# Memory attention and a feed-forward layer on one core: the order of all steps written anew

## The chip, the cores and the metric

One core of a Trainium2 chip runs the whole program. The metric is the device time of one execution in microseconds (us); the number given for a kernel is the median of its runs.

## The reference, cut to what matters

```python
def attention(q, k, v, phi):                 # 8 batches, 8 heads, 576 rows, 64 wide, 32 memories
    a = softmax(phi, axis=2)                 # over the 576 rows
    k_m = einsum('bhsm,bhsd->bhmd', a, k)
    v_m = einsum('bhsm,bhsd->bhmd', a, v)
    attn = softmax((q @ k_m.T) / 8, axis=-1) # over the 32 memories
    return attn @ v_m

def ffn(x, w_in, w_out):                     # x: 4608 x 512, w_in: 512 x 2048, w_out: 2048 x 512
    h = x @ w_in
    return maximum(0.01 * h, h) @ w_out

out = ffn(heads side by side of attention(q, k, v, phi), w_in, w_out)
```

q, k, v and phi are float32. w_in and w_out arrive as 64-bit floating-point numbers.

## The kernel before

**Folding.** The kernel never forms the attention's output. v_m of a batch is multiplied into w_in first (`fold_products`, L896), so that a batch's feed-forward layer takes its 256 attention weights per row straight to the 2048 hidden columns. Operands of most products are split into two float16 parts, and three of the four partial products are kept.

**Named steps.** Every piece of work is a function in the dictionary `steps`, under a short name. Two strings, OPENING (L39) and LATER (L68), list all names once; `run` calls them in that order. No scheduler changes it: each engine (PE, DVE, ACT, POOL, and SP, which issues the transfers) executes its own instructions in the order in which the strings bring them, and waits only for data or for a buffer. Of two steps on different engines, the order in the string means nothing unless one needs the other's result or its buffer.

**The names.** `a0.` to `a7.` are the attention steps of a batch. `phi`, `k`, `v`, `kv0` to `kv3`, `q0`, `q1` load (SP, L535, L546, L566). `A1` (DVE maximum over phi, L575), `A2` (PE transpose, L589), `A3`, `B0`, `B10` (subtract), `B20` (ACT exponential, L620), `B3` (sum), `C10` and `C11` (PE, k_m and v_m, L654), `C2` (PE), `C30` (DVE, L677 to L682), `C3k` (ACT, x_k, L689), `C31` (DVE, x_v, L700), `C4` (DVE, a diagonal of maxima, mdiag, L341), `D10` and `D11` (PE transposes, L719 and L727), `D3` (ACT copy kT, L736), `D2` (PE spread of mdiag, L346), `D4`, `D5`, `D6` (v's scale and its two parts), `Q0`, `Q1` (DVE transposes of q, L772), `E10` and `E1` (PE scores, L793), `E20` to `E22` (DVE transposes out of PSUM, L807), and `S01` to `S18` (softmax over the memories, the chunks 0 and 1).

`i0.` to `i3.` and `o0.` to `o3.` are the quarters of w_in and w_out, each in three pieces of 768, 768 and 512 columns: `ld` (load, L374), `y` and `h` (the high and the low word of the 64-bit number, on ACT, L395 and L384, some `h` on DVE, as OPENING_ACT says), `t` (DVE joins them to float32, L404), `b` (squares for a bound, ACT, L409). Later `k`, `l`, `s`, `m`, `n` split these and their sums into float16.

`f00.` to `f03.` (L909, copied by ACT at L1244) fold the first batch's v_m into a quarter of w_in. `u0.` to `u7.` are eight units of the first group of rows: `P` (PE, L993), `V` (leaky step on ACT, L1000), `O` (PE, L1061). `ci.` and `co.` work out scales of w_in and w_out. `P8` to `P23`, with `V`, `C`, `L`, `O`, are the next two groups; `Wbj` are folded weights (L909, L932, L938). `p0` to `p55` are the units of the remaining fourteen groups: `p` (PE, L1104), `v` (ACT, L1120), `s` (DVE, L1141), `c` (ACT, L1145), `l` (DVE, L1149), and, one or two units later, `d` (PE, L1172). `x` and `z` combine and store.

**Idle products.** `z.4`, `z.1`, `z.3` of the opening (`idle_products`, L1257) are that many 128 by 512 float32 products of ones, whose result nobody reads.

**What limits the order.** PSUM gives the attention steps three banks (`ps_a`), the products `P` and `p` two and the products `O` and `d` three. `ld_slot` (L304) hands out eight buffers in turn, so a load waits until the load eight before it has been worked off. Eight semaphores tell of landings: SP waits with a ninth transfer until the first has landed.

```python
IDLE = (1, 3, 4)

def load(i):                       # one piece of a quarter of w_in or w_out
    c0, n = PIECES[i]
    st = ld_slot().bitcast(I64)
    x = c0
    while x < c0 + n:
        m = min(FQ - x % FQ, c0 + n - x)
        nc.sync.dma_start(st[:, x - c0:x - c0 + m], src[:, x // FQ, x % FQ:x % FQ + m])
        x += m

def squares():
    nc.scalar.activation(junk, dst, AF.Square, scale=SQ_SCALE, accum_out=sq[:, col])
```

Of the kernel before, what the change touches and what calls it, by code (L numbers as in the profile page):

```python
# [45 lines left out]
o1.y0 u1.P1 a0.S16 i2.ld0 o0.t2 a0.S17 u1.V0 u0.O0 a0.S18 i2.ld1 u1.V1 i1.y0 i1.h0 o1.y1 i1.t0  # L46
o1.h0 u1.O0 i1.h1 i1.y1 o1.t0 i1.y2 i1.t1 i2.ld2 i1.h2 u0.O1 o1.h1 i1.t2 i2.h0 i2.y0 o1.t1
o1.y2 i2.t0 o2.ld0 o1.h2 f01.1 i2.y1 i2.h1 u1.O1 o1.t2 f01.2 i2.t1 o2.ld1 o2.ld2 a1.phi i2.y2
i2.h2 o2.y0 u2.P0 i2.t2 a1.kv0 o2.h0 f02.1 u2.V0 o2.t0 o2.y1 a1.kv1 u2.P1 f02.2 u3.P0 a1.kv2
u2.V1 o2.h1 u3.P1 u3.V0 o2.t1 a1.kv3 o2.y2 u2.O0 a1.A1 u3.V1 o2.h2 i1.b a1.q0 o2.t2 a1.A2 u4.P0  # L50
a1.A3 i2.b a1.q1 a1.B0 u4.P1 a1.B10 u4.V0 o0.b u3.O0 i3.ld0 a1.B20 u5.P0 u4.V1 a1.B3 o1.b
a1.C10 u5.V0 o2.b u5.P1 i3.ld1 i3.ld2 o3.ld0 a1.Q0 a1.C2 u2.O1 a1.Q1 u5.V1 i3.y0 a1.C30 i3.h0
a1.C3k u3.O1 a1.C31 i3.y1 i3.h1 a1.C4 i3.y2 i3.h2 i3.t0 a1.D10 a1.D11 i3.t1 a1.D3 a1.D2 u4.O0
a1.D5 a1.D4 o3.y0 i3.t2 o3.h0 i3.b o3.t0 a1.E1 u5.O0 o3.ld1 o3.ld2 a1.E20 a1.E21 a1.S01 a1.E22
a1.S02 a1.S11 ci.1 a1.S03 f03.1 ci.2 a1.S04 a1.S12 o3.y1 ci.3 u4.O1 f03.2 ci.4 e. a1.S05 a1.S13
w0.2 o3.h1 u6.P0 o3.y2 o3.h2 a1.S06 u6.P1 a1.S14 u6.V0 a1.S07 u7.P0 u6.V1 a1.S08 o3.t1 u7.P1
u7.V0 o3.t2 a1.S15 w1.1 o3.b u6.O0 w1.2 u7.V1 a1.S16 co.1 u7.O0 co.2 a1.S17 a1.S18 co.3 u5.O1
# [16 lines left out]
o1.m0 W03.l1 W03.l0 O10.0 V12.0 L11 o0.n3 P12.1 o1.n0 o1.s1 O10.1 V12.1 a2.A3 o1.m1 o1.s2 o1.n1
W13.p o1.m2 C12 a2.B0 o1.s3 W13.h1 P13.0 W13.h0 W13.l1 P13.1 W13.l0 V13.0 o2.k1 L12 P14.0 V13.1
o1.n2 O11.0 o2.k0 o2.l1 V14.0 o2.l0 o2.k2 P14.1 o1.m3 o2.l2 C13 O11.1 V14.1 o1.n3 L13 P15.0
o2.s0 C14 o2.m0 O12.0 o2.s1 V15.0 o2.n0 o2.m1 L14 P15.1 o2.n1 O12.1 o2.s2 V15.1 a2.B10 o2.m2
P16.0 o2.s3 a2.B20 C15 O13.0 o2.n2 V16.0 o3.k0 L15 o3.k1 o3.s0 a2.C10 o3.l0 o3.k2 o2.m3 o3.l1
P16.1 o3.l2 a2.q1 a2.q0 o3.s1 O13.1 V16.1 a2.B3 P17.0 C16 a3.phi a2.C2 o3.s2 V17.0 O14.0 L16
o3.m2 o3.m3 a2.C30 o3.m1 P17.1 o3.n2 a2.C3k o3.n1 O14.1 o3.m0 o3.n3 V17.1 a2.Q0 a2.D10 P18.0  # L80
C17 a2.D3 a2.Q1 O15.0 V18.0 L17 P18.1 a2.C31 i0.l2 a2.E1 V18.1 a2.C4 C18 i0.l1 O15.1 a3.kv3
a3.kv2 a3.kv0 a3.kv1 L18 a2.E20 P19.0 Z1.0 a2.E22 a2.E21 Z1.1 a2.D2 i0.l0 a2.D11 Z1.2 V19.0
a2.S01 O16.0 i1.k0 i1.k1 a2.D4 P19.1 i1.k2 a2.S02 a2.D5 O16.1 V19.1 a2.D6 a2.S03 i1.l2 C19
W20.p i1.l1 P20.0 L19 W20.h0 W20.h1 O17.0 a2.S04 V20.0 P20.1 W20.l0 a2.S05 O17.1 V20.1 C20
a2.S06 P21.0 L20 O18.0 a2.S07 W20.l1 i1.l0 V21.0 a2.S08 P21.1 o2.n3 i2.k0 W21.p V21.1 O18.1
# [6 lines left out]
p2.0 v1.3 Z2.0 os3 p2.1 s1 Z2.2 d0.0 v2.0 d0.1 c1.0 d0.2 v2.1 l1.0 c1.1 p2.2 d0.3 v2.2 l1.1
a3.D5 d0.4 p2.3 a3.D6 a4.A1 a3.E1 v2.3 c2.0 l2.0 d0.5 a4.kv2 a4.kv0 a4.kv3 a4.kv1 d0.6 s2 p3.0
p3.1 v3.0 a3.E20 d1.0 a3.E22 v3.1 c2.1 d1.1 a3.E21 d1.2 l2.1 W30.p p3.2 a3.S01 W30.h0 d1.3 v3.2
W30.h1 d1.4 W30.l0 a3.S02 p3.3 W31.p v3.3 W30.l1 c3.0 d1.5 d1.6 a3.S03 l3.0 p4.0 s3 p4.1 v4.0
d2.0 v4.1 d2.1 a3.S04 c3.1 d2.2 W31.h1 p4.2 d2.3 l3.1 v4.2 W31.h0 d2.4 a3.S05 p4.3 d2.5 v4.3
W31.l0 d2.6 c4.0 W31.l1 p5.0 l4.0 p5.1 v5.0 s4 d3.0 v5.1 d3.1 x3.p a4.A2 a3.S06 d3.2 c4.1 p5.2
l4.1 d3.3 v5.2 a3.S07 d3.4 x3.0 p5.3 x3.1 d3.5 a3.S08 v5.3 x3.2 d3.6 c5.0 a4.A3 p6.0 x3.3 a4.B0
v6.0 l5.0 p6.1 z3.0 d4.0 v6.1 z3.1 d4.1 s5 d4.2 p6.2 a4.B10 c5.1 d4.3 d4.4 v6.2 l5.1 a4.B20
p6.3 d4.5 v6.3 a4.B3 a4.C10 c6.0 l6.0 d4.6 a4.q0 a4.q1 a5.phi s6 a4.C2 p7.0 p7.1 v7.0 a4.C30  # L100
d5.0 v7.1 c6.1 d5.1 a4.C31 d5.2 a4.C3k l6.1 p7.2 a4.D10 v7.2 a4.C4 d5.3 a4.D3 a4.Q0 d5.4 p7.3
a5.A1 d5.5 v7.3 d5.6 c7.0 p8.0 p8.1 l7.0 v8.0 d6.0 s7 v8.1 d6.1 d6.2 a4.Q1 c7.1 p8.2 d6.3 v8.2
a4.D2 l7.1 d6.4 p8.3 a4.D4 a4.D11 v8.3 d6.5 os4 c8.0 W32.p a4.D5 l8.0 d6.6 W32.h1 p9.0 W32.h0
a4.D6 W32.l1 p9.1 v9.0 W32.l0 d7.0 v9.1 s8 a4.E1 x4.p c8.1 d7.1 a5.kv0 a5.kv2 a5.kv1 a5.kv3
l8.1 d7.2 p9.2 x4.0 d7.3 v9.2 a4.E21 d7.4 x4.1 p9.3 x4.2 d7.5 a4.E22 v9.3 d7.6 c9.0 a4.E20
p10.0 x4.3 W33.p l9.0 v10.0 p10.1 s9 W33.h0 d8.0 v10.1 W33.h1 d8.1 W33.l0 c9.1 d8.2 W33.l1
p10.2 l9.1 d8.3 v10.2 z4.1 d8.4 a4.S01 z4.0 p10.3 d8.5 v10.3 W40.p c10.0 d8.6 W40.h1 l10.0
p11.0 W40.h0 s10 p11.1 v11.0 d9.0 v11.1 d9.1 a4.S02 c10.1 d9.2 p11.2 l10.1 d9.3 v11.2 W40.l1
a4.S03 d9.4 W40.l0 p11.3 a4.S04 d9.5 v11.3 W41.p c11.0 d9.6 W41.h1 l11.0 p12.0 W41.h0 s11 p12.1
v12.0 d10.0 v12.1 d10.1 a4.S05 c11.1 d10.2 p12.2 l11.1 d10.3 v12.2 a4.S06 d10.4 p12.3 W41.l0  # L110
d10.5 v12.3 W41.l1 d10.6 c12.0 p13.0 l12.0 a5.A2 v13.0 p13.1 s12 d11.0 v13.1 d11.1 x5.p a5.A3
d11.2 c12.1 p13.2 l12.1 a5.B0 v13.2 d11.3 a4.S07 x5.0 d11.4 p13.3 x5.1 a4.S08 x5.2 d11.5 v13.3
d11.6 c13.0 p14.0 x5.3 p14.1 l13.0 v14.0 d12.0 v14.1 z5.0 d12.1 s13 z5.1 d12.2 p14.2 a5.B10
c13.1 d12.3 d12.4 v14.2 l13.1 a5.B20 p14.3 d12.5 v14.3 a5.B3 a5.C10 c14.0 l14.0 d12.6 a6.phi
a5.q0 a5.q1 s14 a5.C2 p15.0 p15.1 v15.0 a5.C30 d13.0 v15.1 c14.1 d13.1 a5.C31 d13.2 a5.C3k
l14.1 p15.2 a5.D10 v15.2 a5.C4 d13.3 a5.D3 a5.Q0 d13.4 p15.3 a6.A1 d13.5 v15.3 d13.6 c15.0
p16.0 p16.1 l15.0 v16.0 d14.0 s15 v16.1 d14.1 d14.2 a5.Q1 c15.1 a5.D2 p16.2 a5.D11 v16.2 d14.3
l15.1 d14.4 a5.D4 p16.3 d14.5 v16.3 W42.p c16.0 os5 d14.6 W42.h0 l16.0 p17.0 W42.h1 W42.l0
p17.1 v17.0 W42.l1 d15.0 v17.1 s16 d15.1 x6.p a5.D5 d15.2 p17.2 c16.1 x6.0 d15.3 a5.D6 v17.2
l16.1 a5.E1 x6.1 d15.4 a6.kv1 a6.kv0 a6.kv2 a6.kv3 a5.E21 p17.3 x6.2 d15.5 a5.E22 v17.3 d15.6  # L120
c17.0 a5.E20 p18.0 x6.3 W43.p l17.0 v18.0 p18.1 s17 W43.h1 d16.0 v18.1 W43.h0 d16.1 W43.l1
# [1236 lines left out]
```

## Time and profile before

| | us |
|---|---|
| median of 3 runs | 666.64 (666.6 to 666.78) |
| the profiled execution's own time | 668.56 |
| its span, first to last instruction | 666.0 |
| PE busy in the span | 644.3 |
| DVE busy | 515.2 |
| ACT busy | 398.6 |

The profiled execution takes 1.92 us longer than the median, 2.56 us of it outside its span. Differences between two kernels are worked out within the span and then laid on the median. PE is busy almost throughout, so the time is read from the few stretches in which PE stands still or runs at its lower clock, and from what ends them.

### The profile page before, as it was taken

Reading aid. Unit: us, or ns where it says so; the run is one execution under the profiler, and the core shown is the slowest. Engines: PE = TensorE matmul, PEld = TensorE weight load, DVE = VectorE, ACT = ScalarE, POOL = GpSimd, SP = SyncE. Lnnn points to the kernel's source line nnn. Section 1 sums busy time; section 2 is a strip of 40 time slices with the busy share of each in tenths; the row PEclk is TensorE's granted clock in tenths of the full one; section 3 lists DMA queues with packets and bytes.
Section 4 is the critical chain, followed back from the end, with each engine's and each line's share of the span. In section 5 each row is a group of like instructions: output and inputs, shape, how many; then the busy total and the mean of one; then the engine's idle time right before and its main releaser. Section 6 shows DMA issues by size and latency. Waiting matters only on the chain.

```text
span 666.0 us, 17554 instructions
## 1 busy us (share of the span) xinstructions
PE 644.3 (97%) x7592; PEld 483.1 (73%) x7592; DVE 515.2 (77%) x857; ACT 398.6 (60%) x677; POOL 29.8 (4%) x43
## 2 busy tenths in 40 slices
...
GB/s 257 400 317 306 239 170 49 1 1 110 188 1 53 103 144 33 109 144 33 10 132 36 142 1 33 5 104 177 33 14 79 15 33 8 27 20 16 33 2 47
DMA packets 32604, 60.37 MB, mean 91 GB/s; under 512 B 4368, under 2 KB 14608, under 8 KB 32528
## 3 DMA queue, kind: packets, MB, share of 16 engines
...
q8 instruction: 59, 0.97, 0.6%
...
## 4 chain that ended last, share of the span: by engine, by line
PE 84%; DMA 8%; DVE 4%; ACT 1%; SPq 1%; issue 1%; DVEq 0%; ACTq 0%
PE po L1172 28%; PE ph L1104 20%; PE po L1061 13%; PE ph L993 8%; PE ph L1172 5%; PE pa L909 4%; DMA arena<-in_q_dram 3%; PE pa L654 2%; PE pa L793 2%; DMA arena<-in_moe_w_in_dram 2%; PE po L1206 1%; DMA wi<-in_v_dram 1%; DMA arena<-in_phi_dram 1%; DMA arena<-in_moe_w_out_dram 1%; DVE arena L772 1%; DVE r1k L575 1%
## 5 line engine op out<-in xcount | busy, mean ns | idle before, releaser
L1172 PEld LDWEIGHTS <-arena 128*128 128x128 f16 x2184 | 209.8, 98 | 32.0 <-issue 9.0
L1120 ACT ACTIVATE wi<-ph,g_sc 128x256 f32<-128x256 f32 (+1 forms) x224 | 99.8, 465 | 167.2 <-PE ph L1104 166.3
L1104 PE MATMUL ph<-a,w_mem 128*128 128x256 f16 (+3 forms) x1440 | 147.1, 247 | 3.3 <-ACT wi L1120 3.1
L1104 PEld LDWEIGHTS <-w_mem 128*128 128x128 f16 x1440 | 115.4, 98 | 18.3 <-issue 6.7
L1172 PE MATMUL po<-wo,arena 128*128 128x256 f16 x936 | 122.5, 273 | 0.0
L1172 PE MATMUL po<-arena 128*128 128x256 f16 x936 | 121.9, 273 | 0.0
L1061 PE MATMUL po<-wo,arena 128*128 128x512 f16 (+1 forms) x384 | 110.7, 434 | 0.0
L1149 DVE TENSOR_TENSOR arena<-arena 128x1024 f16<-128x1024 f32 x52 | 63.2, 1216 | 27.7 <-ACT arena L1145 27.6
L1149 DVE TENSOR_TENSOR arena<-wi,arena 128x768 f16<-128x768 f32 (+1 forms) x60 | 52.9, 882 | 31.5 <-ACT arena L1145 31.3
L1145 ACT CAST arena<-arena 128x1024 f16<-128x1024 f32 x52 | 54.2, 1043 | 10.5 <-DVE arena L1141 10.2
L993 PE MATMUL ph<-a,w_mem 128*128 128x192 f16 (+2 forms) x304 | 53.8, 323 | 1.7 <-DVE a L852 1.7
L1141 DVE TENSOR_TENSOR arena<-wi 128x256 f32<-128x256 f32 x104 | 39.2, 418 | 15.3 <-ACT wi L1120 15.3
L1061 PEld LDWEIGHTS <-arena 128*128 128x128 f16 x288 | 27.8, 98 | 29.3 <-issue 0.9
L1145 ACT CAST arena<-wi 128x768 f16<-128x768 f32 (+1 forms) x60 | 46.5, 775 | 1.8
L1141 DVE TENSOR_TENSOR arena<-wi,arena 128x256 f32<-128x256 f32 x104 | 43.8, 422 | 1.8
L1172 PE MATMUL ph<-wo,arena 128*128 128x256 f16 x312 | 42.6, 273 | 0.0
L876 POOL TENSOR_TENSOR a<-t,a 128x384 f16<-128x384 f32 x22 | 21.4, 997 | 450.9 <-ACT a L871 380.4
L1061 PEld LDWEIGHTS po<-wo,arena 128*128 128x128 f32 x96 | 17.6, 190 | 21.0 <-issue 19.1
L772 DVE STREAM_TRANSPOSE arena<-arena 96x1536 f32<-96x1536 f32 x14 | 24.7, 1766 | 8.0 <-DMA arena<-in_q_dram 3.7
L1000 ACT ACTIVATE arena<-ph,g_sc 128x384 f32<-128x384 f32 x32 | 18.5, 578 | 18.3 <-PE ph L993 17.6
L909 PE MATMUL pa<-wi,vT 64*32 64x512 f16 (+1 forms) x704 | 29.0, 420 | 0.4 <-ACT vT L742 0.4
L993 PEld LDWEIGHTS <-w_mem 128*128 128x128 f16 x240 | 20.8, 98 | 9.3 <-issue 2.7
...
## 6 DMA issues: line engine op xcount, KB each, us to landing
...
```

The costliest lines, as they stand in the source:

```text
L772: nc.vector.transpose(flat, ld["q", g].rearrange("p hh j d -> p (hh j d)"))
L876: nc.gpsimd.tensor_tensor(lo[:, tb], t2[:, tb], hi[:, tb], ALU.subtract)
L909: nc.tensor.matmul(pf[g][cols, :], lhs, rhs, start=(n == 0), stop=(n == len(passes) - 1), tile_position=(g * D, hh * M),)
L993: nc.tensor.matmul(ph[:, t0:t0 + n * SB], lhs, rhs, start=(m == 0), stop=(m == len(seq) - 1))
L1000: nc.scalar.activation(dst, ph, AF.Prelu, scale=sc, alpha=SLOPE)
L1061: nc.tensor.matmul(po, lhs, rhs, start=(f == 0 and m == 0), stop=(f == NQ * NF - 1 and m == len(seq) - 1),)
L1104: nc.tensor.matmul(ph[:, t0:t0 + n], lhs, rhs, start=(m == 0), stop=(m == len(seq) - 1))
L1120: nc.scalar.activation(dst, ph, AF.Prelu, scale=g_sc2[:, j:j + 1], alpha=SLOPE)
L1141: nc.vector.tensor_tensor(gt[:, x], y, z, op)
L1145: nc.scalar.copy(dst[:, 0], src)
L1149: nc.vector.tensor_tensor(dst[:, 1], src, dst[:, 0], ALU.subtract)
L1172: nc.tensor.matmul(acc, g[:, x, s, u], rhs, start=(h == 0 and j == 0 and u == 0 and m == 0), stop=(j == NQ - 1 and u == 1 and m == 2), ski ...
```

## The change

Only the two strings and IDLE change. No step is taken away or altered; the one new step is `z.2`, two idle products behind `f00.1` and ahead of `u0.P0`. The core of the diff:

```diff
 OPENING = """
-z.4 a0.phi0 a0.phi1 a0.k a0.q0 a0.A10 a0.A11 a0.A2 a0.q1 a0.A3 a0.B0 z.1 a0.B10 a0.B11 a0.B20
-i0.ld0 a0.B21 a0.C10 a0.B3 i0.ld1 a0.C2 z.1 a0.C30 i0.ld2 a0.Q0 a0.C3k a0.v a0.D10 a0.D3 a0.Q1
-a0.E10 i0.y0 a0.E1 z.3 o0.ld0 i0.h0 a0.E20 i0.y1 a0.E21 i0.t0 o0.ld1 i0.h1 a0.S01 i0.y2 i0.h2
-i0.t1 o0.ld2 a0.S02 o1.ld0 i0.t2 a0.S03 a0.C11 a0.E22 i0.b a0.S11 a0.C31 o1.ld1 a0.S12 a0.D11
-a0.S04 a0.D5 a0.S13 f00.1 o1.ld2 o0.y0 a0.S05 f00.2 i1.ld0 a0.S06 o0.y1 a0.C4 u0.P0 o0.h0
-a0.S14 i1.ld1 a0.D2 o0.h1 u0.P1 o0.t0 u0.V0 a0.D4 a0.S15 o0.y2 i1.ld2 u1.P0 u0.V1 o0.t1 o0.h2
...
+a0.phi0 z.4 z.1 a0.phi1 a0.k a0.q1 a0.A10 a0.A11 a0.A2 a0.q0 a0.A3 a0.B0 a0.B10 a0.B11 a0.B20
+a0.B21 a0.C10 i0.ld1 z.1 a0.B3 a0.C2 i0.ld0 i0.ld2 a0.C30 a0.C3k a0.D10 a0.D3 a0.Q0 a0.E10 a0.v
+o0.ld0 a0.Q1 i0.y0 o0.ld2 a0.E1 z.3 a0.E22 a0.S11 i0.h0 i0.t0 i0.y1 i0.y2 i0.h1 i0.t1 i0.h2
+o0.ld1 i1.ld0 o1.ld0 a0.E20 a0.E21 a0.S01 a0.S02 a0.S03 a0.S12 a0.S13 a0.C11 o1.ld2 a0.C31
+a0.D11 i0.t2 a0.D5 f00.1 a0.S04 z.2 f00.2 a0.S05 a0.S06 i1.y0 u0.P0 u0.V0 i0.b o0.y0 o0.h0
+o1.y0 a0.C4 a0.D2 u0.P1 a0.S14 o0.y1 o0.t0 o1.ld1 o0.y2 i1.ld1 o0.h2 u1.P0 i1.ld2 a0.S15 u0.V1
+a0.S16 a0.D4 u0.O0 o0.t2 a0.S17 a0.S18 o0.h1 u1.V0 i1.h0 i1.t0 u1.P1 u1.V1 o1.h0 o0.t1 i1.h1
...
+u4.P0 a1.B0 o2.h2 a1.B10 i2.b o0.b u4.P1 u4.V1 u3.O0 o2.t2 i3.ld0 a1.q0 a1.B20 a1.B3 a1.C10
+a1.Q1 u2.O1 u5.P0 o1.b i3.ld2 u4.V0 i3.ld1 a1.C2 a1.C30 a1.C3k i3.y2 u5.V0 u5.P1 u5.V1 i3.y0
+u3.O1 o2.b a1.C31 a1.C4 a1.D11 i3.h0 a1.D5 a1.D10 a1.D3 i3.y1 o3.ld0 o3.y0 o3.h0 i3.h2 a1.Q0
+a1.D2 a1.D4 i3.h1 a1.E1 i3.t1 i3.t0 i3.t2 i3.b a1.E20 a1.E22 a1.E21 a1.S11 u4.O0 a1.S01 a1.S02
+o3.ld1 o3.y1 f03.1 ci.1 o3.t0 o3.h1 u5.O0 a1.S03 u4.O1 a1.S12 f03.2 a1.S04 a1.S13 ci.2 ci.3
...
+a1.S15 o3.h2 o3.t1 u6.P1 u6.V1 o3.t2 u6.O0 a1.S16 w1.2 o3.b co.1 a1.S17 u7.O0 co.2 co.3 a1.S18
...
-IDLE = (1, 3, 4)
+IDLE = (1, 2, 3, 4)
 
 LATER = """
...
-a3.q1 a3.q0 a4.phi a3.C2 v0.3 O22.1 a3.C30 c0.0 s0 a3.C3k p1.0 a3.D10 l0.0 v1.0 c0.1 p1.1
-a3.C31 O23.0 l0.1 v1.1 a3.D3 a3.Q0 a3.D11 p1.2 O23.1 a3.C4 v1.2 a3.Q1 a3.D2 Z2.1 p1.3 a3.D4
...
+c0.0 s0 O22.1 a3.q0 l0.0 c0.1 a3.C2 l0.1 p1.0 a3.q1 p1.1 v1.0 a3.C30 O23.0 v1.1 a3.C3k a3.C31
+a3.Q0 a4.phi a3.D10 a3.D11 a3.C4 a3.D3 p1.2 O23.1 a3.Q1 v1.2 a3.D2 Z2.1 p1.3 a4.A1 p2.0 v1.3
...
+c15.0 s15 a5.q1 p16.0 p16.1 v16.0 l15.0 d14.0 v16.1 a5.C31 c15.1 d14.1 a6.phi d14.2 a5.C3k
+l15.1 p16.2 a5.D10 v16.2 a5.Q0 a5.D11 a5.D3 d14.3 d14.4 a5.C4 p16.3 a5.Q1 a5.D2 v16.3 d14.5
...
```

In the opening, the pieces of w_in's first quarter are now loaded in the order 1, 0, 2. In LATER, the rows of the plan up to `W23` keep PE's order; behind them, q of a batch is loaded as `q0`, `q1` and then the next batch's phi, the step `A1` of the next batch stands behind the scores `E1`, and within a unit the cast `c` of the second half stands behind the next unit's first two `v`.

## Rows read from the trace of the kernel before

**Rows 1.** The page: busy time by engine, and the engines' shares of the chain

```profile
PE 644.3 (97%) x7592; PEld 483.1 (73%) x7592; DVE 515.2 (77%) x857; ACT 398.6 (60%) x677; POOL 29.8 (4%) x43
...
PE 84%; DMA 8%; DVE 4%; ACT 1%; SPq 1%; issue 1%; DVEq 0%; ACTq 0%
```

**Rows 2.** Stretches: PE, PEld, DVE, ACT, POOL busy, PEclk, DMA share, GB/s

```profile
29.00:33.00 4.00, 3.31 (x7) 2.14 (x8) 2.94 (x9) 3.00 (x6) 1.38 (x1) 0.60 1.03 402
33.00:37.00 4.00, 4.00 (x13) 2.26 (x13) 3.01 (x6) 3.07 (x6) 0.22 (x1) 0.97 1.04 405
224.00:228.00 4.00, 3.44 (x20) 2.37 (x18) 3.48 (x11) 1.64 (x4) 0.00 (x0) 0.57 0.03 7
...
340.00:360.00 20.00, 18.25 (x224) 16.19 (x222) 15.86 (x27) 11.02 (x21) 0.00 (x0) 1.00 0.27 70
```

**Rows 3.** Waits of PE (us, times, longest), then its timeline after the opening

```profile
PE ph L1104 <- ACT wi L1120: 5.3, 7, 1.8
...
223.46 0.49 PE L346 MATMUL pa<-mdiag,ones 128*128 128x128 f32 x2 [2.15 <-DVE mdiag L341]
...
352.90 0.33 PE L1104 MATMUL ph<-a,arena 128*128 128x128 f16 x3 [1.75 <-ACT wi L1120]
...
521.75 0.81 PE L1104 MATMUL ph<-a,w_mem 128*128 128x256 f16 x6 [1.29 <-ACT wi L1120]
```

**Rows 4.** Timeline of PE in the opening: start, duration, work, idle before

```profile
6.98 0.27 PE L589 MATMUL pa<-ident,r1k 128*128 128x128 f32 x1
...
20.04 2.84 PE L1260 MATMUL pa<-ones 128*128 128x512 f32 x6 [0.64 <-DVE t L807]
...
29.69 2.76 PE L993 MATMUL ph<-a,w_mem 128*128 128x384 f32 x4 [1.73 <-DVE a L852]
...
48.35 1.45 PE L993 MATMUL ph<-a,w_mem 128*128 128x384 f32 x4
49.73 1.09 PE L909 MATMUL pa<-wi,vT 64*32 64x512 f32 x16
...
74.26 2.74 PE L1061 MATMUL po<-wo,arena 128*128 128x512 f32 x6
76.93 1.96 PE L793 MATMUL pa<-arena,kT 32*32 32x192 f32 x96
...
83.62 0.38 PE L487 MATMUL pa<-diag,ones 4*128 4x4 f32 x2 [0.83 <-DVE diag L481]
```

**Rows 5.** Timeline of ACT in the opening

```profile
16.53 0.90 ACT L395 ACTIVATE arena<-arena 128x768 f32<-128x768 f32 x1 [0.64 <-DMA arena<-in_moe_w_in_dram]
19.68 0.91 ACT L395 ACTIVATE arena<-arena 128x768 f32<-128x768 f32 x1 [1.48 <-DMA arena<-in_moe_w_in_dram]
20.49 0.93 ACT L384 ACTIVATE arena<-arena 128x768 uint32<-128x768 uint16 x1
...
24.67 1.89 ACT L409 ACTIVATE wi<-wi 128x2048 bf16<-128x2048 f32 x1
...
32.48 0.49 ACT L1000 ACTIVATE arena<-ph 128x384 f32<-128x384 f32 x1 [1.00 <-PE ph L993]
...
71.26 0.73 ACT L689 ACTIVATE x_k<-pa,r 128x192 f32<-128x192 f32 x2 [1.54 <-DVE r L682]
```

**Rows 6.** Timeline of DVE in the opening

```profile
22.07 0.95 DVE L404 SCALAR_TENSOR_TENSOR wi<-arena 128x768 uint32<-128x768 uint32 x1
...
28.56 0.98 DVE L852 STREAM_TRANSPOSE a<-t 128x768 f32<-128x768 f32 x1
```

**Rows 7.** Groups of ACT by form, 33 to 76 us: busy us, mean ns

```profile
L384 ACT ACTIVATE arena<-arena 128x512 uint32<-128x512 uint16 x6 | 4.0, 673 | 0.0
...
L1244 ACT COPY w_mem<-pa 128x512 f32<-128x512 f32 x4 | 2.1, 580 | 0.3 <-PE pa L909 0.3
```

**Rows 8.** Timeline of DVE: Q0 of two attention steps, with the idle before

```profile
220.88 1.77 DVE L772 STREAM_TRANSPOSE arena<-arena 96x1536 f32<-96x1536 f32 x1 [2.89 <-DMA arena<-in_phi_dram]
...
345.25 1.77 DVE L772 STREAM_TRANSPOSE arena<-arena 96x1536 f32<-96x1536 f32 x1 [2.22 <-DMA arena<-in_q_dram]
```

More of the change, by code (lines that the diff above doesn't have):

```diff
@@ L46 @@
[L46 to L57, printed above, removed]
```

223 lines of the change are left out of this document (113 added, 110 removed).

## The prediction

> **What bounds the kernel now.** The page comes first: PE is busy for 97% of the span, and 84% of the chain that ended last lies on it [rows 1]. No step is removed, so only PE's standing still and its lower clock can give time, and only new standing can cost any. Next I read the stretches for the clock. Two show half of it: 29 to 33 us (granted 0.60, then 0.97) and 224 to 228 us (0.57) [rows 2]; 0.40 and 0.43 of 4 us lost are about 1.7 us each. Each follows a wait of PE: 1.73 us ahead of 29.69 [rows 4], 2.15 us ahead of 223.46 [rows 3]. The stretch 340 to 360 us kept a clock of 1.00 [rows 2] in spite of a wait of 1.75 us [rows 3]. Last come PE's waits, in two kinds: seven of `p` for `v` (5.3 us, the last of them, 0.44, at the very end, so 4.9 can be had), and 2.15 for mdiag [rows 3]. Both kinds go back to q: in each attention step, Q0 stands on DVE until its transfer lands (2.89 and 2.22 us [rows 8]), and what is queued behind it, `s`, `l` and mdiag, comes late, with the `c` and `v` that need their buffers.
>
> **The opening, part by part.** I walked the two orders engine by engine, laying each operation's duration of before on the new order.
>
> (1) z.1 goes ahead of A2. Before, A2 starts at 6.98 with no wait, straight behind z.4 [rows 4]. z.1 is two matmuls, and six take 2.84 [rows 4], so it costs 0.9 on the chain A2, A3, B, C10; the other z.1, now ahead of C2, 0.1 to 0.2. The scores end 1.0 later.
>
> (2) i0.ld1 is issued before i0.ld0, while ACT still takes `y0` first. Before, y0 started at 16.53 and y1 at 19.68, each released by its transfer [rows 5]. If the transfers land in the order of issue, y0 starts at 19.7. ACT then has y0, h0, y1, y2, h1 at a spacing of 0.81 [rows 5], and h1 ends at 23.6; before it ran from 20.49 to 21.42 [rows 5]. On DVE t0 and t1 (0.95 each [rows 6]) now stand ahead of E20; the last transpose S06, which ended at 29.54 [rows 6], and t2 behind it end at 31.7, and u0.P0 starts at 31.9 instead of 29.69 [rows 4].
>
> (3) z.2 stands in just that gap. Two products are four matmuls, 1.9 us by the same six in 2.84 [rows 4], from 29.9 to 31.8: free, as PE had nothing else. P0 took 2.76 at half clock, the same four matmuls 1.45 elsewhere [rows 4]. So P0 ends at 33.3 rather than 32.45: 0.9 behind. If the cover is gone (D5 or f00.1 late), the 1.9 lies on the path; that is in the upper bound.
>
> (4) ACT becomes the limit behind u0.V0. In the new order i0.b (1.89 [rows 5]), which ran in ACT's free time at 24.67, stands behind V0. From 33.3 to i2.h2 ACT has four V of 0.48 [rows 5] (1.9), i0.b 1.9, one cast of V's size 0.5, f01.2 1.05 (two copies of 0.58, overlapping [rows 7]), eleven words of 768 columns at 0.85 (9.35) and eight of 512 at 0.6 (4.8; alone 0.67 [rows 7]). That is 19.5, to 52.8. With i2.t2 (0.7) behind it f02.1 starts at 53.5; before it started at 49.73 [rows 4]. So 3.8 behind. On the way PE, ready for u0.O0 at 36.4, waits 2.0 for o0.t0, for V0, i0.b, o0.y0, o0.h0 (0.5 + 1.9 + 1.7) and the join end at 38.4.
>
> (5) From there to C3k the chain B20, C10, u2.O1, u5.P0, C2, C30 keeps its length. C3k started at 71.26 and ended by 72.0 [rows 5]; now 75.7. Then ACT has i3.y2 0.6, two V 1.0, i3.y0 0.85, o2.b 1.9, D5 0.3, D3 0.55: 5.2, so kT is there at 80.9. PE has C2, u5.P1, u3.O1 and the small steps D10, D11, D2 until 79.0 and waits 2.0 for E1. E1 starts at 81.0 with u4.O0 (2.74 [rows 4]) still to do, where before it started at 76.93 with u4.O0 done [rows 4]: 81.0 + 2.7 − 76.9 = 6.8 behind.
>
> (6) ci.3's wait of 0.83 [rows 4] goes, since ci.2 has more work in front. co.1 waits about 1.0 for o3.b, which has two V, two words and w1.2's join ahead of it. Sum of the opening: 6.8 − 0.8 + 1.0 = **+7.0**. Bounds: 5 where ACT's words come at their spacing of 0.81 rather than 0.85 and piece 0 lands a matmul or two sooner; 10 where z.2 is no longer covered and both waits grow by what ACT's queue holds.
>
> (7) Clock. The waits of 2.0 (u0.O0, E1) have no counterpart in the trace; the nearest are 2.15 (clock fell, 1.7 lost) and 1.75 (it did not) [rows 2, 3]. 2.0 is nearer to 2.15, but u0.O0's wait comes soon after the idle products. I take one fall, +1.7; bounds 0 and 3.4. z.2 saves the fall at 29.69, which is inside the 0.9 of (3) already.
>
> **LATER.** (8) Until W23 PE keeps its order and nothing waits in either: 0. (9) Then q0, q1 are loaded ahead of the next phi, A1 (some 2 us on DVE) stands behind E1, and the late `c` stands behind the next two `v`, so that ACT serves PE first. What goes: 2.15 for mdiag, the 4.9 of `v`, and the 1.7 of the clock at 224 that followed the 2.15: **−8.7**. (10) What comes: in a5 and a7 Q0 (1.77 [rows 8]) now stands ahead of C4 on DVE, so mdiag is later by it. PE's other units cover some; the bounds are 0 and 1.77 each, and I take 0.7, as the C30 chain ends 9.9 us behind C10 and PE comes to D2 after 9.2. In a6, C31 stands ahead of C4 (0.6, bounds 0 and 0.85). In a3, D6 stands behind `s` and `l`: E1 waits 0 to 1.2, I take 0. Sum **+2.0**, bounds 0 and 3.5.
>
> **Sum.** 7.0 + 1.7 − 8.7 + 2.0 = +2.0. The profiled execution took 668.56 us for a span of 666.0; laid on the median, 666.64 + 2.0 = **668.6 us**.
>
> **The rivals.** *A, faster:* the first quarter's pieces land as early as before, and ACT keeps up. The sum (2) hangs on the order of landing. For it: piece 1's own 3.15 us behind piece 0 [rows 5] is long for equal pieces, so part of it may belong to the start of a piece, not to its size, and y0 would start 1.5 sooner. Against: y0 and y1 were each released by their own landing, in order of issue [rows 5]. Then the opening is +5.3, without the clock's fall, and where LATER's new waits find cover, 666.6 + 5.3 − 8.7 = 663.2. [...]
>
> *B, no change:* both waits of 2.0 leave the clock alone, as the 1.75 did [rows 2, 3]: 668.6 − 1.7 = 666.9.
>
> *C, slower by more:* both waits in the opening drop the clock (+1.7 again), and (10) is at its upper bound (+1.5): 671.8. It decides where PE stands 2.0 or more at u0.O0.
>
> *D, the change does not do what it says:* q, though issued before phi, still lands too late for Q0, because the eight landing semaphores hold SP back, and D2 and `v` wait as before for a half of the 8.7: 668.6 + 4.4 = 673.0. Against it stands Q0 at 220.88, released by phi, the transfer behind q [rows 8].
>
> **How the numbers follow.** A measurement of this kernel tells 0.2%, 1.33 us, from no change. The forecast has a chance of 0.34, its own range 667 to 671; A 0.34; B 0.18, C 0.10, D 0.04. Forecast, C and D are slower: 0.48; B is the same: 0.18; A faster: 0.34. A goes down to 661 where the opening's lower bound of 5 meets the full 8.7 and the last waits go too. The range from 662 to 672.5 leaves out D, the upper part of C, and A's lower end.
>
> **What would show it.** In the changed profile: y0 at 19.7 released by the transfer (2); P0 at 31.9 with about 1.45 for four matmuls, and a granted clock near 1.00 in 29 to 33 (3); waits of PE near 2.0 for o0.t0 (L404) ahead of u0.O0, and for kT (L736) ahead of E1 at 81 (4, 5); the opening's last product some 7 us later than before; a clock below 0.7 in one 4-us stretch near 83 (7); no wait for q in front of a Q0, the waits of `p` for `v` down from 5.3 to under 1 (9); two or three waits for mdiag of under 1 us in their place (10). The prediction is wrong if y0 starts before 18.5, if E1 starts before 79, or if the waits for `v` remain.

## The result, and the profile after

The changed kernel takes 671.03 us (median of 4 runs, 670.82 to 673.06) against 666.62 before on the same chip: a ratio of 1.0079 (95% interval 1.0054 to 1.0104), 4.4 us slower. A second comparison on another chip gave 1.0107 (1.0077 to 1.0136). The prediction was 668.6 with a range of 662 to 672.5: the direction is right, the time lies in the range, and the step is more than twice the 2.0 us forecast. The profiled execution has a span of 668.8 us, 2.8 above that of before. Executions over 1.5% longer than the fastest of the same kernel are left out of the medians and counts here: one of e7's twelve and three of e10's.

The waits of PE in the changed kernel, from the page of waits (us in total, times, longest), show what came and what went [rows 3]:

```profile
PE pa L727 <- DVE x_v L700: 2.5, 2, 1.6
PE pa L793 <- ACT kT L736: 2.5, 2, 1.8
PE po L1061 <- DVE wo L404: 2.2, 1, 2.2
PE po L654 <- ACT wi L620: 1.7, 1, 1.7
PE pa L654 <- issue: 1.5, 1, 1.5
PE pa L719 <- ACT x_k L689: 1.5, 1, 1.5
PE po L1061 <- ACT arena L384: 1.3, 1, 1.3
PE pa L469 <- ACT wi L409: 1.1, 1, 1.1
PE ph L1104 <- ACT wi L1120: 1.0, 2, 0.6
...
PE pa L346 <- DVE mdiag L341: 0.8, 2, 0.4
```

The waits of `p` for `v` fell from 5.3 to 1.0 us and the one for mdiag from 2.1 to 0.8. In their place stand waits for words of w_in and w_out and for kT in the opening, and one inside a C10 with no releaser ("issue"). The waits for ACT's exponential (L620) and for x_k, and 1.56 us of those for x_v, lie ahead of u0.P0, where the new opening is not behind yet. PE's timeline in the opening, the rows that answer to [rows 4]:

```profile
30.99 1.53 PE L993 MATMUL ph<-a,w_mem 128*128 128x384 f32 x4
...
37.54 2.84 PE L1061 MATMUL po<-wo,arena 128*128 128x512 f32 x6 [2.21 <-DVE wo L404]
...
42.99 5.39 PE L1061 MATMUL po<-wo,arena 128*128 128x512 f32 x12 [1.32 <-ACT arena L384]
...
53.64 1.65 PE L909 MATMUL pa<-wi,vT 64*32 64x512 f32 x16 [0.18 <-DVE wi L404]
...
81.34 1.93 PE L793 MATMUL pa<-arena,kT 32*32 32x192 f32 x96 [1.84 <-ACT kT L736]
83.20 2.84 PE L1061 MATMUL po<-wo,arena 128*128 128x512 f32 x6
...
93.08 0.38 PE L487 MATMUL pa<-diag,ones 4*128 4x4 f32 x2 [0.53 <-DVE diag L481]
...
103.66 0.27 PE L469 MATMUL pa<-ident,sq 128*4 128x128 f32 x1 [1.05 <-ACT wi L409]
```

u0.P0 (30.99) ends at 32.52, where before it ended at 32.45 [rows 4]: up to there the new opening costs nothing. f02.1 is 3.9 us behind, E1 4.4 and with u4.O0 still to do 7.15. The waits at 37.54, 42.99, 81.34 and 103.66 us alone come to 6.4 us. The first work of LATER on PE (the first fold, L909) starts 7.96 behind, before and in the changed kernel:

```profile
106.71 1.09 PE L909 MATMUL pa<-wi,vT 64*32 64x512 f32 x16
```

```profile
114.67 1.09 PE L909 MATMUL pa<-wi,vT 64*32 64x512 f32 x16
```

The whole ends 2.8 behind, so LATER gives back 5.2 in these two traces. The stretches of the changed kernel:

```profile
29.00:33.00 4.00, 3.94 (x15) 2.00 (x13) 3.28 (x8) 2.33 (x5) 0.33 (x1) 1.00 1.03 400
33.00:37.00 4.00, 2.32 (x8) 1.04 (x6) 0.48 (x1) 4.00 (x6) 0.50 (x1) 1.00 0.58 224
224.00:228.00 4.00, 4.00 (x26) 2.42 (x25) 3.07 (x8) 2.41 (x6) 0.00 (x0) 1.00 1.09 258
```

In 33 to 37 us ACT is busy for all of the 4.00 us, while PE has 2.32 and DVE 0.48: ACT is the limit there, as step (4) had it. The granted clock (the third column from the right) is 1.00 in all three, and 0.999 over this execution, where the profiled one of before had 0.60 and 0.57 [rows 2].

**How much of the 4.4 is the clock.** Each execution's mean granted clock and span are known. The 81 executions of before taken beside the experiments had clocks of 0.990 to 1.000 (median 0.995) and a median span of 664.7; the nine at 0.998 or more lie at 661.2 to 663.2, median 662.0. The profiled one, 666.0 at 0.994, was thus 1.3 us above the usual. The changed kernel's eleven (those above and e11's) had 0.986 to 0.999, nine of them 0.990 or less, and a median span of 671.0; its two at 0.998 or more had 668.8 and 667.2. At full clock the change costs about 6 us, by the medians of the spans 6.3. The clock alone does not settle the time: at 0.986 to 0.990 the changed kernel's spans lay at 668.7 to 670.9 in the first comparison and at 671.0 to 673.2 in the second. "At full clock" below means a mean clock of 0.998 or more.

### The profile page after: what moved, and what is told of

The parts are those of the page before. It is cut to its first block, busy times and chain, and to the rows that moved or that the text cites. A ratio compares the mean times of both kernels' runs of the same rounds, so it can differ in the third digit from the quotient of the medians.

```text
span 668.8 us, 17618 instructions
## 1 busy us (share of the span) xinstructions
PE 642.7 (96%) x7596; PEld 482.1 (72%) x7596; DVE 521.6 (78%) x857; ACT 395.1 (59%) x677; POOL 32.3 (5%) x43
## 4 chain that ended last, share of the span: by engine, by line
PE 83%; DMA 5%; ACT 5%; DVE 4%; issue 1%; SPq 0%; ACTq 0%; DVEq 0%
PE po L1172 29%; PE ph L1104 20%; PE po L1061 12%; PE ph L993 6%; PE ph L1172 5%; PE pa L909 4%; DMA arena<-in_moe_w_in_dram 3%; PE pa L654 2%; PE pa L793 2%; ACT arena L395 1%; PE po L1206 1%; DVE arena L772 1%; DMA arena<-in_q_dram 1%; DMA arena<-in_moe_w_out_dram 1%; ACT wi L409 1%
## 5 line engine op out<-in xcount | busy, mean ns | idle before, releaser
L1104 PE MATMUL ph<-a,w_mem 128*128 128x256 f16 (+3 forms) x1440 | 145.0, 246 | 0.7 <-ACT wi L1120 0.6
L993 PE MATMUL ph<-a,w_mem 128*128 128x192 f16 (+2 forms) x304 | 52.4, 317 | 0.1
L1141 DVE TENSOR_TENSOR arena<-wi,arena 128x256 f32<-128x256 f32 x104 | 46.4, 446 | 1.8
L876 POOL TENSOR_TENSOR a<-t,a 128x384 f16<-128x384 f32 x22 | 23.8, 1104 | 455.5 <-ACT a L871 455.5
L1000 ACT ACTIVATE arena<-ph,g_sc 128x384 f32<-128x384 f32 x32 | 18.6, 580 | 21.0 <-PE ph L993 20.3
L909 PE MATMUL pa<-wi,vT 64*32 64x512 f16 (+1 forms) x704 | 29.6, 420 | 0.9 <-ACT vT L742 0.7
```

What stands on the lines that cost most here:

```text
L876: nc.gpsimd.tensor_tensor(lo[:, tb], t2[:, tb], hi[:, tb], ALU.subtract)
L909: nc.tensor.matmul(pf[g][cols, :], lhs, rhs, start=(n == 0), stop=(n == len(passes) - 1), tile_position=(g * D, hh * M),)
L993: nc.tensor.matmul(ph[:, t0:t0 + n * SB], lhs, rhs, start=(m == 0), stop=(m == len(seq) - 1))
L1000: nc.scalar.activation(dst, ph, AF.Prelu, scale=sc, alpha=SLOPE)
L1104: nc.tensor.matmul(ph[:, t0:t0 + n], lhs, rhs, start=(m == 0), stop=(m == len(seq) - 1))
L1141: nc.vector.tensor_tensor(gt[:, x], y, z, op)
```

## The experiments

The two strings can be exchanged one by one. First each half alone.

**e1, the old OPENING with the changed LATER**

```diff
-a0.phi0 z.4 z.1 a0.phi1 a0.k a0.q1 a0.A10 a0.A11 a0.A2 a0.q0 a0.A3 a0.B0 a0.B10 a0.B11 a0.B20
...
+z.4 a0.phi0 a0.phi1 a0.k a0.q0 a0.A10 a0.A11 a0.A2 a0.q1 a0.A3 a0.B0 z.1 a0.B10 a0.B11 a0.B20
...
-IDLE = (1, 2, 3, 4)
+IDLE = (1, 3, 4)
```

> The order of before in OPENING (without z.2), the changed order in LATER. Theory (the opening costs about 8 us, LATER gives back about 5): the opening ends at 106.7 us again, and the gain of LATER is left alone. In the traces the changed LATER is 5.2 us shorter, of which 1.7 is the lower clock at 224 us; so 661.4 us, or 663.1 if ordinary executions of before have no such fall. Rival (LATER gains only because a later opening moves its loads to a better place): about 666.

Measured: 662.99 us (6 runs), ratio 0.9921 (0.9897 to 0.9945); one execution at full clock, 659.1, 2.9 less than before's 662.0. By the ratio the gain is 5.3 us, the theory's first figure (661.4); against the 667.49 of before beside it, 4.5; at full clock it is nearer to the second (663.1). The two figures are not told apart, but the rival's 666 is out: LATER's gain does not need the late opening.

**e2, the changed OPENING with the old LATER**

```diff
-a2.phi a2.kv3 a2.kv1 W01.h0 W01.h1 i0.k0 W01.l1 a2.kv2 W01.l0 i0.k1 o0.s0 Z0.0 a2.A1 Z0.1 W11.p
...
+a2.kv1 a2.phi a2.kv2 a2.kv3 a2.kv0 W01.h1 W01.h0 i0.k1 W01.l0 i0.k0 W01.l1 i0.k2 o0.s0 Z0.0
...
```

> The changed OPENING with z.2, the order of before in LATER. Theory: the opening alone costs 8.0 us and nothing of it is given back, so 674.6 us, with the waits for q at 228, 353 and 528 us as before. Rival (the loss of the opening is swallowed by the waits for q, as q has more time to land): 669 or less.

Measured: 677.06 (4 runs), ratio 1.0127 (1.0090 to 1.0163), 8.5 us by the ratio. The theory holds: nothing of the opening's loss is swallowed. This profile also shows a lower clock behind the wait ahead of E1 (stretches, then PE's timeline):

```profile
80.00:84.00 4.00, 1.70 (x66) 1.36 (x70) 2.21 (x5) 4.00 (x7) 0.00 (x0) 0.88 0.06 21
84.00:88.00 4.00, 4.00 (x58) 2.04 (x35) 3.62 (x7) 3.24 (x4) 0.00 (x0) 0.50 0.39 82
88.00:92.00 4.00, 4.00 (x23) 1.20 (x22) 2.02 (x3) 2.04 (x5) 2.70 (x2) 0.77 0.95 364
```

```profile
82.62 2.92 PE L793 MATMUL pa<-arena,kT 32*32 32x192 f32 x96 [2.30 <-ACT kT L736]
85.47 5.00 PE L1061 MATMUL po<-wo,arena 128*128 128x512 f32 x6
```

PE waited 2.30 us, then ran at a granted clock of 0.50 (84 to 88 us): u4.O0 took 5.00 us instead of 2.84. The fall of step (7) is there in this execution and absent from the profiled one of the changed kernel, whose clock stays at 1.00 from 80 to 92 us.

**e3, without z.2**

```diff
-a0.D11 i0.t2 a0.D5 f00.1 a0.S04 z.2 f00.2 a0.S05 a0.S06 i1.y0 u0.P0 u0.V0 i0.b o0.y0 o0.h0
+a0.D11 i0.t2 a0.D5 f00.1 a0.S04 f00.2 a0.S05 a0.S06 i1.y0 u0.P0 u0.V0 i0.b o0.y0 o0.h0
```

> The changed kernel without z.2. Theory: u0.P0 runs at half clock again (about 2.8 us instead of 1.5) but starts no sooner, since S06 releases it; u0.O0's wait of 2.2 us for o0.t0 behind it swallows the 1.3 us, so 671.0 within 0.5. Rival 1 (z.2 is worth what it saves of the clock): 672.3 or more. Rival 2 (z.2 itself is on the path): 669 to 670.

Measured: 672.73 (7 runs), ratio 1.0066 (1.0043 to 1.0089), not to be told from the changed kernel's 1.0079 and 1.0107. PE's timeline:

```profile
32.49 2.90 PE L993 MATMUL ph<-a,w_mem 128*128 128x384 f32 x4 [2.33 <-DVE a L852]
...
40.38 1.98 PE L1061 MATMUL po<-wo,arena 128*128 128x512 f32 x4 [2.10 <-DVE wo L404]
```

P0 takes 2.90 us where the changed kernel has 1.53, at a granted clock of 0.88 in 29 to 33 us and 0.69 in 33 to 37. It also starts 1.5 us later than in the changed kernel, but in this execution the clock was already low from 8 to 28 us (0.82 over the first 29), so that is not z.2's doing. And the wait for o0.t0 stays at 2.10 instead of falling to 0.9: V0, ahead of i0.b and o0.y0 on ACT, waits for P0 and comes later by as much. The theory's mechanism was wrong, and no price of z.2 can be told from this run.

**e4, the pieces in order again**

```diff
-a0.B21 a0.C10 i0.ld1 z.1 a0.B3 a0.C2 i0.ld0 i0.ld2 a0.C30
+a0.B21 a0.C10 i0.ld0 i0.ld1 z.1 a0.B3 a0.C2 i0.ld2 a0.C30
```

> The changed kernel with i0.ld0 issued ahead of i0.ld1 again. Theory: y0 starts near 16.5 instead of 18.65, t1, S01 and x_v on DVE come about 1 us sooner (x_v then waits for C11, which ends at 25.3), so u0.P0 and all of ACT behind it come 1.0 us sooner: 670.0. Rival (ACT's own queue between V0 and f02.1 is the limit whatever comes ahead, or the transfers behind it are): no change, 671.0.

Measured: 671.77 (12 runs), ratio 1.0056 (1.0033 to 1.0079); four executions at full clock, 665.7 to 667.5 (mean 666.8). y0 starts at 16.51 instead of 18.65, P0 at 30.59 instead of 30.99: 0.4 of the 1.0 expected at P0, about 1.2 at the end, in intervals that overlap. Likely a small part of the loss, not shown beyond that.

**e5, o2.b behind kT's copy**

```diff
-u3.O1 o2.b a1.C31 a1.C4 a1.D11 i3.h0 a1.D5 a1.D10 a1.D3 i3.y1
+u3.O1 a1.C31 a1.C4 a1.D11 i3.h0 a1.D5 a1.D10 a1.D3 o2.b i3.y1
```

> The changed kernel with o2.b moved on ACT from ahead of kT's copy (a1.D3) to behind it. Theory (ACT's order is what holds E1): the wait of 1.84 us for kT ahead of E1 is gone (below 0.3), and the opening and the whole are 1.8 us shorter where the clock is the same: a span of 667.0 at full clock (668.8 for the changed kernel). Rival (ACT is simply short of time there, so the 1.9 us come back further on): the wait at E1 goes, those for diag and for i3.b at 93 and 104 us grow by as much, span 668.8.

Measured: 671.05 (10 runs), ratio 1.0057 (1.0032 to 1.0083); three at full clock, 666.2 to 667.4. PE's timeline:

```profile
79.04 1.92 PE L793 MATMUL pa<-arena,kT 32*32 32x192 f32 x96 [0.65 <-DVE arena L772]
...
84.95 1.55 PE L909 MATMUL pa<-wi,vT 64*32 64x512 f32 x16 [1.22 <-DVE t L807]
```

The wait for kT is gone, and two follow: E1 now waits 0.65 for Q0, and f03.1 1.22 for the transposes that free its PSUM bank. Part of what E1 gains is lost again at f03.1: the first fold of LATER starts at 113.44, 1.2 us sooner than in the changed kernel's profile above and 0.55 sooner than in e11's. At full clock the gain is about 1.2 (a mean of 666.8 in three against 668.0 in two). Neither the theory's 1.8 nor the rival's 0.

**e6, i0.b back in ACT's gap**

```diff
-a0.D11 i0.t2 a0.D5 f00.1 a0.S04 z.2 f00.2 a0.S05 a0.S06 i1.y0 u0.P0 u0.V0 i0.b o0.y0 o0.h0
+a0.D11 i0.t2 a0.D5 i0.b f00.1 a0.S04 z.2 f00.2 a0.S05 a0.S06 i1.y0 u0.P0 u0.V0 o0.y0 o0.h0
```

> The changed kernel with i0.b ahead of f00.1, in the gap that ACT has near 28 us, instead of behind u0.V0. Theory (ACT is the limit behind V0, and i0.b is 1.9 us of it): u0.P0 starts as before near 31.0, the wait ahead of u0.O0 falls from 2.2 to 0.3, and what follows comes 1.9 us sooner: a span of 666.9 at full clock. Rival (the words of w_out are limited by their landings, or ACT catches up by itself further on): the waits at 42 and 53 us grow, span 668.5 or more.

Measured: 668.99 (10 runs), ratio 1.0030 (1.0005 to 1.0056). PE's timeline:

```profile
36.24 2.84 PE L1061 MATMUL po<-wo,arena 128*128 128x512 f32 x6 [0.35 <-DVE wo L404]
41.71 5.39 PE L1061 MATMUL po<-wo,arena 128*128 128x512 f32 x12 [1.34 <-ACT arena L384]
52.61 1.65 PE L909 MATMUL pa<-wi,vT 64*32 64x512 f32 x16 [0.43 <-DVE wi L404]
...
80.28 2.58 PE L793 MATMUL pa<-arena,kT 32*32 32x192 f32 x96 [1.82 <-ACT kT L736]
82.78 3.80 PE L1061 MATMUL po<-wo,arena 128*128 128x512 f32 x6
```

The wait at u0.O0 falls from 2.21 to 0.35, as expected; f02.1 comes 1.0 earlier, not 1.9, as a wait of 0.43 appears there and the 1.3 at 42 us stays. Behind the wait for kT the clock fell in this execution (granted 0.67 in 80 to 84 us, 0.91 in 84 to 88): E1 takes 2.58 us instead of 1.93 and u4.O0 3.80 instead of 2.84, 1.6 us lost, so that the first fold of LATER starts at 114.54, no sooner than the changed kernel's 114.67. None of the ten executions is at full clock (0.992 to 0.997). By the ratio this is the largest gain of a single move, 1.0030 against 1.0056 and 1.0057 of e4 and e5, though the intervals overlap. Whether the shorter wait or the clock makes it is not shown.

**e7, the kernel before with z.2**

```diff
-f00.2 i1.ld0 a0.S06 o0.y1 a0.C4 u0.P0 o0.h0
+f00.2 i1.ld0 a0.S06 o0.y1 a0.C4 z.2 u0.P0 o0.h0
```

> The kernel before, with z.2 ahead of u0.P0 and nothing else. Theory: at full clock it costs 0.2 us (the two products end at 29.9, P0 was released at 29.7); executions in which the clock fell at P0's wait gain 1.1 to 1.3 us, so its mean clock is higher and the median lies 0 to 1 us lower than before. Rival (the clock falls elsewhere instead, or falls whatever PE does): the clock's spread over the executions stays as for before, 0.991 to 1.0, and the median is 0.2 higher.

Measured: 666.26 (11 runs), ratio 1.0002 (0.9974 to 1.0029); full clock 662.2 to 663.5, clocks 0.992 to 1.0. In its profile P0 takes 1.45 us instead of 2.76, yet the clocks spread as before. The idle products are worth nothing that could be measured; this settles neither account.

**e9, the three moves of e4, e5 and e6 together**

```diff
-a0.B21 a0.C10 i0.ld1 z.1 a0.B3 a0.C2 i0.ld0 i0.ld2 a0.C30
+a0.B21 a0.C10 i0.ld0 i0.ld1 z.1 a0.B3 a0.C2 i0.ld2 a0.C30
...
-a0.D5 f00.1 a0.S04 z.2 f00.2 a0.S05 a0.S06 i1.y0 u0.P0 u0.V0 i0.b o0.y0
+a0.D5 i0.b f00.1 a0.S04 z.2 f00.2 a0.S05 a0.S06 i1.y0 u0.P0 u0.V0 o0.y0
...
-u3.O1 o2.b a1.C31 a1.C4 a1.D11 i3.h0 a1.D5 a1.D10 a1.D3 i3.y1
+u3.O1 a1.C31 a1.C4 a1.D11 i3.h0 a1.D5 a1.D10 a1.D3 o2.b i3.y1
```

> The changed kernel with three moves of its opening undone together: i0.ld0 ahead of i0.ld1, i0.b in ACT's gap near 28 us, o2.b behind kT's copy. Theory (the opening's loss lies in these three, and they add): 1.0 + 1.9 + 1.2 = 4 us less than the changed kernel, a span near 664.8 at full clock, where the old opening with the changed LATER has 659.1; the rest, some 5 us, lies in the order of PE and DVE. Rival (they cover one another, as all of them feed the same queue of ACT): 666.5 or more.

Measured: 668.36 (12 runs), ratio 1.0024 (1.0005 to 1.0044); three at full clock, 664.6 to 665.2. At full clock that is about 3.2 below the 668.0 (the mean of 668.8 and 667.2) of the changed kernel, where e4 and e5 alone gave about 1.2 each and e6 has no execution. This fits the theory of adding without showing it: by the ratio, the three (1.0024) are not to be told from e6 alone (1.0030). Of the opening's loss of 8.9 at full clock (668.0 less the 659.1 of e1), some 5.7 is left in the order of the other steps. The waits of 1.33 (42 us), 1.19 (f03.1) and 1.05 (co.1) in its profile are part of it; how the rest divides was not tried.

**e11, the changed kernel again.** No edit.

> The changed kernel itself, unaltered, to have more of its executions beside those of before on one chip. Theory: median ratio 1.006 to 1.008; at full clock a span of 668.5 to 669, some 6.5 us above that of before (662.0), since the executions of before at full clock lack the two falls of the profiled one; its own executions at 0.986 to 0.988 some 2 us longer. Rival (the first four executions were high by chance): 1.004 or less, 666.5 at full clock.

Measured: 673.66 (7 runs), ratio 1.0107 (1.0077 to 1.0136), on the chip of e9; one at full clock, 667.2, the six others 0.986 to 0.990 with spans of 671.0 to 673.2. The theory's direction holds, its median ratio was too low, its 668.5 at full clock 1.3 too high, and the others are 4 to 6 us longer, not 2.

**e8, a hybrid:** the opening of before with z.2 ahead of u0.P0 and the changed LATER, in it C4 ahead of Q0 for batches 5 and 7 (the first pair of lines stands against before, the others against the changed kernel).

```diff
-a0.S04 a0.D5 a0.S13 f00.1 o1.ld2 o0.y0 a0.S05 f00.2 i1.ld0 a0.S06 o0.y1 a0.C4 u0.P0 o0.h0
+a0.S04 a0.D5 a0.S13 f00.1 o1.ld2 o0.y0 a0.S05 f00.2 i1.ld0 a0.S06 o0.y1 a0.C4 z.2 u0.P0 o0.h0
...
-l15.1 p16.2 a5.D10 v16.2 a5.Q0 a5.D11 a5.D3 d14.3 d14.4 a5.C4 p16.3 a5.Q1 a5.D2 v16.3 d14.5
+l15.1 p16.2 a5.D10 v16.2 a5.C4 a5.Q0 a5.D11 a5.D3 d14.3 d14.4 p16.3 a5.Q1 a5.D2 v16.3 d14.5
...
-v36.0 l35.0 d34.0 v36.1 a7.C31 c35.1 d34.1 a7.D11 a7.C3k d34.2 l35.1 p36.2 a7.Q0 a7.D10 v36.2
-d34.3 a7.D3 d34.4 a7.C4 p36.3 a7.Q1 a7.D2 v36.3 d34.5 c36.0 d34.6 s36 p37.0 p37.1 v37.0 l36.0
+v36.0 l35.0 d34.0 v36.1 a7.C31 c35.1 d34.1 a7.D11 a7.C3k d34.2 l35.1 p36.2 a7.C4 a7.Q0 a7.D10
+v36.2 d34.3 a7.D3 d34.4 p36.3 a7.Q1 a7.D2 v36.3 d34.5 c36.0 d34.6 s36 p37.0 p37.1 v37.0 l36.0
```

> The opening of before with z.2, the changed LATER, and in it C4 ahead of Q0 again for batches 5 and 7. Theory: the two waits of 0.4 us for mdiag go, 0.8 less than the old opening with the changed LATER, so a span of 658.5 at full clock and a ratio to before of 0.990. Rival (C4 ahead of Q0 makes Q0, and with it E1 and the softmax, late, and a wait for s or v takes their place): 659.3 or more, as the kernel without the two moves (659.1 at a clock of 0.999).

Measured: 660.49 us (6 runs, 659.89 to 662.23), ratio **0.9909** (0.9877 to 0.9940); four at full clock, 657.6 to 658.6. It beats both kernels: 6.1 us less than before by the ratio. The waits for mdiag that step (10) foresaw are gone and nothing took their place. After W23 PE stands still three times for over 0.3 us, the last of them at the very end as before; PE's timeline has the other two:

```profile
223.76 0.82 PE L1104 MATMUL ph<-a,w_mem 128*128 128x256 f16 x6 [0.56 <-ACT wi L1120]
...
269.43 2.18 PE L654 MATMUL pa<-arena 64*32 64x128 f32 x136
273.09 0.42 PE L654 MATMUL pa<-arena 64*32 64x128 f32 x8 [1.49 <-issue]
```

**e10 and e12, the stall inside C10.** In all the runs above with the changed LATER PE stands inside batch 4's C10 for 1.2 to 1.5 us, with no wait shown; in before that C10 takes 2.25 us without a break. To move the place, 80 small products took the place of z.2 (e10: all written to one place of PSUM; e12: to four groups of columns).

```diff
+        if n == 2:
+            for _ in range(40):
+                nc.tensor.matmul(
+                    pi[:32, 0, :], ones[:64, :32], ones[:64, :], start=True, stop=True
+                )
+            return
```

> The hybrid, with 80 small products (64 rows, 32 by 128) in the place of the four of z.2, so that PE's program is 76 matmuls longer ahead of batch 4's C10. In every kernel with the changed LATER PE stands 1.2 to 1.5 us inside that C10 with no wait shown, after 136 of its 144 matmuls with z.2 and after 140 without it. Theory (PE runs out of loaded program at a fixed place in it, and C10's matmuls, 16 ns each, use it up faster than it comes): the place moves to 60 of 144, the stall there shrinks to 0.3 or less, the span is 1.2 to 1.5 us shorter than the hybrid's 658.0, unless the same thing appears in another C10. Rival (C10 itself waits, for data or for the load of q issued at that time): the stall stays after the 136th matmul, span 658.

> As the kernel with 80 small products in the place of z.2, but spread over four column groups of PE, where the 80 before it wrote one and took 111 ns each (8.9 us in all, 5.9 of them on the path). Theory: they take some 2.3 us, at most 0.4 more than z.2 on the path, the stall inside batch 4's C10 is gone as in that kernel (C10 2.25 us instead of 4.1), and the span is 656.9 at full clock, 1.1 below the hybrid's 658.0. Rival (the stall went there only because everything was 6 us later): C10 takes 3.8 us or more again, span 658.4.

Measured: e10 666.48 (9 runs), ratio 0.9987 (0.9966 to 1.0007); e12 662.15 (6), ratio 0.9907 (0.9883 to 0.9932), two at full clock, 658.0 and 658.3. PE's timeline of e10, then of e12:

```profile
28.29 8.89 PE L1261 MATMUL pa<-ones 64*32 64x128 f32 x80
...
275.20 2.25 PE L654 MATMUL pa<-arena 64*32 64x128 f32 x144
```

```profile
28.83 4.52 PE L1262 MATMUL pa<-ones 64*32 64x128 f32 x80
33.28 2.93 PE L993 MATMUL ph<-a,w_mem 128*128 128x384 f32 x4
...
273.39 2.25 PE L654 MATMUL pa<-arena 64*32 64x128 f32 x144
```

The stall is gone from that C10 in both, at times of the run (273.39 and 275.20) between those of two kernels that have it (269.43 in e8, 276.70 in the changed kernel). So it hangs on the place in PE's program, not on C10's data or on q's load. At full clock e12 equals e8, and the gain of 1.1 does not show in the whole. It is there in LATER alone: from its first fold (at 107.40 us in e8, 111.36 in e12, 113.18 in e10) to the end it is 551.7 us in e8, 550.3 in e12 and 549.9 in e10. What was won there went into the small products ahead, which in e12's profile came at a granted clock of 0.50 (29 to 37 us); there batch 1's C10 also has a new stall of 0.33 us.

## Why the prediction was right, and where it was off

**Right.** The chain through ACT: (4) f02.1 at 53.5 (measured 53.64) with a wait of 2.0 ahead of u0.O0 (2.21), though the 53.5 is luck in part, as ACT came to u0.V0 0.7 us sooner (32.56 for 33.3) and then stood 1.63 us for a transfer of w_in ahead of 49.36; (5) kT's wait of 2.0 (1.84) and E1 at 81.0 (81.34), with u4.O0 behind it; co.1's wait for o3.b, 1.0 (1.05). (6) The sum of the opening was +7.0 and is +7.96. (3) z.2 fitted its gap, and P0 ran at full clock (1.00 in 29 to 33 us). (9) The waits for `v` went from 5.3 to 1.0. (10) The waits for mdiag in a5 and a7 are there, 0.40 and 0.42 instead of 0.7; a6 has none for mdiag but one of 0.96 at D11 for x_v, which e11's trace of the same kernel does not have. e8 shows that the two for mdiag come from Q0 ahead of C4. e1 and e2 show the two halves separately, and e6 and e5 that i0.b and o2.b are behind the two long waits.

**Off by small sums that cancel.** (1) z.1 cost nothing: the scores ended at 19.36 as before (19.40), since E1's second half, with an "issue" pause of 0.43 in it, took 2.03 us before and 1.21 now. (2) y0 started at 18.65, not 19.7: in both traces the first two pieces landed in the order of issue, 3.1 us apart (16.5 and 19.6 before, 15.5 and 18.6 now), and both came 1.0 sooner. That part of this interval belongs to a piece's start, as rival A argued, is not shown; A's larger part fell, as e4 brings y0 back to 16.51 and gains about 1 us at most. (6) ci.3's wait did not go (0.53 of 0.83), and a wait of 1.32 for a word of w_out at 42 us was not foreseen. (10) The upper bound of 3.5 is not the sum of its parts' bounds, which is 5.6; what was measured, 1.8, lies below both.

**The step that failed is the sum's "the 1.7 of the clock at 224" and, in part, the 2.15 with it, in (9).** They were priced from one execution. The fall is a matter of the execution: e7, with the same LATER as before, shows D2's wait at 0.86 us and no fall (a mean clock of 0.999), and e2, also with it, 1.61 and no fall (1.00 from 220 to 240 us). Two executions without a fall, whose LATER starts at the same place, compare best, e7's and e1's:

```profile
105.82 1.09 PE L909 MATMUL pa<-wi,vT 64*32 64x512 f32 x16
```

```profile
105.85 1.09 PE L909 MATMUL pa<-wi,vT 64*32 64x512 f32 x16
```

Their spans are 662.8 and 659.1, so LATER's change gives 3.7 us, not 6.7 (4.1 by the full-clock executions of e7 and e8, 4.9 apart, less the 0.8 of the two waits for mdiag that e8 lacks); 1.5 of the difference is the C10 stall, which no row of before showed. Laying a difference of spans on the median was the second error: before's profiled execution took 1.9 us more than the median (668.56 and 666.62), the changed kernel's 0.1 less. In the traces and medians, the way from the forecast +2.0 to +4.4 is thus: opening +1.0 (7.96 for 7.0), the fall of (7) −1.7, LATER +1.5 (5.2 given back for 6.7), and +1.6 from the executions to the medians. That the two traces differ by 2.8, near the 2.0, is in part luck.

**Partly right: (7).** The fall after the new waits, +1.7, was absent from the profiled execution and present at E1 in e2's and e6's, in e6 at 1.6. The length of the wait alone does not decide it: 1.82 us ahead of E1 was followed by a fall in e6 (0.67 in 80 to 84 us) and by none in e3 and e4 (1.00 from 80 to 92). The clocks of the executions (0.986 to 0.990 in nine of eleven, against a median of 0.995) fit more and longer falls in the changed kernel. An earlier place, which the prediction did not reckon with, comes out of the kept traces: in e2, e3 and e9, three of the eight with this opening, the clock is low from 8 to 28 us (0.82 over the first 29 in each), ahead of both long waits, as in this stretch of e9:

```profile
20.00:24.00 4.00, 3.32 (x27) 1.20 (x6) 3.23 (x4) 1.99 (x3) 1.51 (x2) 0.50 1.04 399
```

With z.1 moved ahead of A2, PE stands still for 1.7 us ahead of C10 and 1.5 ahead of D10, where before it had 0.63 and 0.65. That this lowers the clock was not tried; e4, e5, e6 and e11 have the same waits and no fall there (1.00 over the first 29 us), and e8, with the opening of before, is low from 16 us on (0.88 over the first 29). In which stretches the clock fell in executions without a trace stays open.
